# A linear-attention and gated MoE-style kernel: order of work listed anew, three sums moved to TensorE, four transfers moved to ScalarE's queue

## The chip, the cores and the metric

One core of one Trainium2 chip runs the whole program. The time is device microseconds of that core for one execution. Three executions of the kernel before took 303.40 to 303.96 us, median 303.87.

## The reference

Two stages follow each other. Inputs are float32 as the core sees them for the first stage; the weights of the second (`w_in`, `conv_w`, `w_out`) come as float64 and are split on the chip into a high and a low part.

```python
# first stage: 4 batches, 8 heads, 768 steps, head size 48
f = 1.0 / (1.0 + np.exp(-f_logit))
for t in range(S):
    state = f[:, :, t, :, None] * state + np.einsum('bhd,bhe->bhde', k[:, :, t], v[:, :, t])
    y[:, :, t] = np.einsum('bhd,bhde->bhe', q[:, :, t], state)
x = y.transpose(0, 2, 1, 3).reshape(B, S, 384)
# second stage
h = np.maximum(x @ w_in, 0.0)                       # 384 -> 1024
conv_out = sum(conv_w[k] * hp[:, k:k + S, :] for k in range(3))   # hp: h padded by one step
out = (h * (1.0 / (1.0 + np.exp(-conv_out)))) @ w_out            # 1024 -> 384
```

## The kernel before, in words

The steps of a batch are cut into six chunks of 128, so there are 24 chunks, numbered n; half a batch (three chunks, 384 steps) is the unit of the second stage, and there are eight of those, numbered u.

A chunk needs the running sum of the logarithms of its gates. The gates come in groups of three chunks. For the groups in `CFG["cg"]` they are loaded with time on the partitions (L493), ScalarE takes the logarithm (L505, L509), and TensorE sums by four matmuls with a triangle of ones (`cumulate`, L530). For the other groups the load has features on the partitions (L495) and VectorE runs a scan along time (L537). Two exponentials of the sum follow on ScalarE (L539, L541), and VectorE multiplies keys and queries by them (L545). TensorE then computes scores in four quarters of its array (L567), transposes the keys (L560), and multiplies keys by values (L595) and masked scores by values (L587). VectorE copies the scores through the mask (L575) and carries the state (L608, L611), which ScalarE decays (L617). TensorE adds queries times state (L631), and ScalarE and VectorE write the result as a high part and a remainder (L644, L646) into the tile `xT` of the half batch.

Heads have 48 rows of 64, so a quarter of each output would stay empty. Six gap transfers in each half batch (L654), from SBUF to SBUF, fill the gaps with rows of a fourth slot. They wait for the last remainder (L646) of the half batch, and the projection of the half batch waits for all six.

The second stage of a half batch: nine matmuls for each of eight blocks of `w_in` (L684, high and low parts), a halved relu (L694), three taps of the convolution (L700, L704), a tanh (L708), the product (L710), a split into high and low (L727, L731), 24 matmuls with `w_out` (L740), a copy (L746) and a store (L748).

The weights are split beside the first chunks by VectorE and ScalarE (`split_f64`, L390 to L436); two splits let TensorE join the parts by matmuls with the identity (L431 to L433), and the first projection waits for two of the three splits of `w_in`. In the end the weights are loaded once more to check that none is out of range (L760 to L766), and the count of good ones (L781, L782) decides on a slow path that does not run here.

Every step is an operation with needs, buffers and engine (`plan.op`). `ORDER`, a table of operation numbers, sets the sequence of each engine; `order` walks it with modelled times and hands out the buffers (`rings`) as they come free. All transfers are issued by SP, in the table's order; each waits for the transfer eight places ahead of it. In the model, `told`, `edge`, `asked` and `read` count TensorE's instructions against the places at which a new block of 256 has to be there. Before the sequence begins, seven matmuls on a zeroed tile keep TensorE busy (`STIR`, L368).

Of the kernel before, what the change touches and what calls it, by code (L numbers as in the profile page):

```python
# [11 lines left out]
F32 = mybir.dt.float32  # L12
# [40 lines left out]
845 716 809 722 367 120 123 797 379 836 323v 339 353 851 326 370 819 340 824 399 350 341 397 798 398 787 342 351 400  # L53
# [35 lines left out]
class Plan:  # L89
# [34 lines left out]

    def buf(self, i):
        return self.at[i]

    def order(self):
        now = 0.0
        free = {e: 800.0 for e in self.LAT}  # L130
# [21 lines left out]
        while events:  # L152
# [18 lines left out]
            for e in free:  # L171
# [8 lines left out]
                for o in [o for o in todo[e][:1] if o in ready[e]] if turn else sorted(ready[e], key=lambda o: o.key):  # L180
# [5 lines left out]
                    for r, i in o.take:  # L186
                        if not turn and r not in self.LOOSE and fifo[r][head[r]] is not o:
                            ok = False
                            break
# [768 lines left out]
```

## Time and profile before

| what | value |
|---|---|
| median of 3 executions | 303.87 us |
| the profiled execution | 303.62 us |
| its span, first to last instruction | 301.9 us |
| TensorE matmuls | busy 287.8 us, 95% |
| TensorE weight loads | busy 271.6 us, 90% |
| VectorE | busy 255.9 us, 85% |
| ScalarE | busy 243.4 us, 81% |
| GpSimd | busy 28.1 us, 9% |
| moved by transfers | 43.57 MB, mean 144 GB/s |

The profiled execution took 303.62 us; its span is 1.72 us shorter, which lies around the program's own instructions. PE is TensorE (PEld its weight loads), DVE is VectorE, ACT is ScalarE, POOL is GpSimd, and a q behind an engine's name stands for its sequencer, which waits and issues transfers. A float32 matmul is recorded as two passes, a transpose or a reduced-precision one as one. In the chain of waits, each row is what released the next; "issue" there, and as a releaser, is time for which the profile shows nothing that was waited for.

### The profile page before, as it was taken

What the parts mean: (1) busy time and instruction counts of PE and PEld (TensorE: products, weight loads), DVE (VectorE), ACT (ScalarE), POOL (GpSimd) and SP (SyncE); (2) the same over time, 40 slices, a digit from 0 to 9 for tenths busy, and PEclk for the clock granted to TensorE, in tenths of its full rate; (3) what the DMA queues carried; (4) which work ended last, traced back from release to release, by engine and by line L of the source; (5) the groups of instructions that cost most, each with busy time, mean ns of one, the idle gap of its engine ahead of it and who ended that gap; (6) DMA issues with size and microseconds to landing.
All of it is one profiled execution on the core that took longest, in us unless ns stands there. A gap on an engine that the chain in (4) does not pass through costs nothing.

```text
span 301.9 us, 10060 instructions
## 1 busy us (share of the span) xinstructions
PE 287.8 (95%) x4281; PEld 271.6 (90%) x4281; DVE 255.9 (85%) x394; ACT 243.4 (81%) x457; POOL 28.1 (9%) x72
## 2 busy tenths in 40 slices
PE   7668979999999999999999999999999999999994
PEld 6557667999999999999999999999999999999993
DVE  5959999999999999999999789995886698479530
ACT  6959788999678799899999778678989795796521
POOL 4003240002110010012000000020000002000000
PEclk9979999999999999999999999999999999999999
DMA  6996899542510344744361433553643505201211
GB/s 209 391 407 227 259 270 374 169 124 72 154 44 7 121 134 125 218 138 136 100 196 62 145 90 104 143 169 107 204 144 99 148 29 143 69 26 41 80 38 58
DMA packets 19476, 43.57 MB, mean 144 GB/s; under 512 B 2764, under 2 KB 9700, under 8 KB 19428
## 3 DMA queue, kind: packets, MB, share of 16 engines
q1 hardware_dynamic: 19428, 42.90, 44.3%
q8 instruction: 34, 0.56, 0.8%
q14 instruction: 14, 0.11, 0.1%
HBM read 35.81 MB, written 4.72 MB: 134 GB/s over the span
## 4 chain that ended last, share of the span: by engine, by line
PE 87%; DVE 5%; DMA 3%; issue 2%; SPq 1%; ACT 0%; DVEq 0%; ACTq 0%
PE mm L684 34%; PE mm L740 33%; PE Y L587 4%; PE S L567 3%; PE Y L631 3%; PE Y L595 3%; PE Y L560 3%; DVE kq L545 2%; DMA xT<-xT 2%; DMA xT<-in_moe_conv_w_dram 1%; SPq L654 1%; DVE ob L423 1%; DVE fb L537 1%; PE mm L530 1%; PE mm L431 1%
## 5 line engine op out<-in xcount | busy, mean ns | idle before, releaser
L684 PE MATMUL mm<-xT,wi 128*128 128x384 f32 x576 | 107.7, 341 | 1.5 <-DMA xT<-xT 1.5
L684 PEld LDWEIGHTS mm<-xT,wi 128*128 128x128 f32 x576 | 100.5, 188 | 2.9 <-ACT e L539 1.7
L704 DVE SCALAR_TENSOR_TENSOR g<-hb,cw,g 128x384 f32<-128x384 f32 (+1 forms) x128 | 73.5, 614 | 6.0 <-ACT g L700 5.6
L740 PE MATMUL mm<-wo,gh 128*128 128x384 f32 x384 | 71.0, 338 | 0.0
L740 PEld LDWEIGHTS mm<-wo,gh 128*128 128x128 f32 x384 | 66.4, 188 | 0.5 <-ACT gh L727 0.2
L700 ACT ACTIVATE g<-hb,cw 128x384 f32<-128x384 f32 (+1 forms) x64 | 37.8, 618 | 2.6 <-DVE gl L731 2.1
L694 ACT ACTIVATE hb<-mm 128x384 f32<-128x384 f32 x64 | 31.2, 488 | 10.7 <-PE mm L684 10.1
L731 DVE TENSOR_TENSOR gl<-g,gh 128x1024 fp32r<-128x1024 f32 (+2 forms) x28 | 29.6, 1067 | 10.8 <-ACT gh L727 7.2
L740 PE MATMUL mm<-wo,gl 128*128 128x384 f32 x192 | 37.4, 338 | 0.0
L740 PEld LDWEIGHTS mm<-wo,gl 128*128 128x128 f32 x192 | 33.3, 188 | 0.1
L727 ACT CAST gh<-g 128x1024 fp32r<-128x1024 f32 (+2 forms) x28 | 26.1, 938 | 7.8 <-PE mm L740 6.3
L710 DVE SCALAR_TENSOR_TENSOR g<-g,hb 128x768 f32<-128x768 f32 (+1 forms) x32 | 30.3, 956 | 1.7 <-ACT g L708 1.6
L708 ACT ACTIVATE g<-g 128x768 f32<-128x768 f32 (+1 forms) x32 | 27.0, 845 | 3.7 <-DVE g L704 3.6
L545 DVE TENSOR_TENSOR kq<-kq,e 128x1024 f32<-128x1024 f32 x24 | 29.1, 1216 | 0.1
L587 PE MATMUL Y<-am,v 64*48 64x64 f32 (+1 forms) x768 | 23.5, 219 | 2.5 <-issue 2.5
L543 POOL COPY ft_all<-e 128x4 f32<-128x4 f32 x24 | 14.1, 592 | 104.1 <-ACT e L541 104.0
L537 DVE TENSOR_TENSOR_SCAN fb<-runs,fb 128x512 f32<-128x512 f32 x18 | 21.8, 1217 | 0.4 <-ACT fb L509 0.3
L746 ACT COPY ob<-mm 128x384 f32<-128x384 f32 x24 | 11.4, 474 | 12.5 <-PE mm L740 6.3
L567 PE MATMUL S<-kq 48*64 48x64 f32 x768 | 16.9, 222 | 3.3 <-DVE kq L545 3.3
L575 DVE COPY_PREDICATED am<-mask,S 128x512 f32<-128x512 uint8 x24 | 17.6, 733 | 2.8 <-PE Y L587 2.8
L646 DVE TENSOR_TENSOR xT<-Y,xT 112x512 fp32r<-112x512 f32 x24 | 16.5, 687 | 2.5 <-ACT xT L644 2.4
L567 PEld LDWEIGHTS S<-kq 48*64 48x64 f32 x768 | 13.9, 134 | 5.2 <-DVE kq L545 3.7
(95 smaller groups left out, 362.2 us busy)
## 6 DMA issues: line engine op xcount, KB each, us to landing
kq<-in_kq_dram SPq DMA_DIRECT2D x24, 512.0 KB, 4.4
fb<-in_f_logit_dram SPq DMA_DIRECT2D x18, 256.0 KB, 4.8
v<-in_v_dram SPq DMA_DIRECT2D x24, 192.0 KB, 4.2
out_dram<-ob SPq DMA_DIRECT2D x24, 192.0 KB, 2.1
kq<-in_moe_w_out_dram SPq DMA_DIRECT2D x8, 384.0 KB, 3.7
kq<-in_moe_w_in_dram SPq DMA_DIRECT2D x6, 512.0 KB, 4.4
xT<-xT SPq DMA_DIRECT2D x48, 48.0 KB, 2.9
xT<-in_moe_w_in_dram SPq DMA_DIRECT2D x4, 512.0 KB, 7.9
```

The lines of the kernel that those rows point to most:

```text
L545: ox = plan.op("DVE", 1222, lambda e, X=X, E=E: nc.vector.tensor_tensor(buf(X), buf(X), buf(E), ALU.mult), ka, need=[o2, ld_x], use=[X, E])
L567: o = nc.tensor.matmul(scores()[t, j, p, :], buf(X)[r, 0, p, t], buf(X)[r, 1, p, t], start=True, stop=True)
L587: o = nc.tensor.matmul(out_of(Y, p, j, w, z), buf(V).rearrange("p h d -> p (h d)")[t, h * D:h * D + w], buf(AM)[t, j, p, :], start=x == 1 ...
L684: nc.tensor.matmul(buf(ph)[:, :HS], wi[:, t, wl, f * P:(f + 1) * P], x_view(pl, u)[:, t, xl, :], start=(i == 0), stop=(i == 3 * KT - 1))
L694: nc.scalar.activation(hb[:, 2:HS + 2], buf(ph)[:, :HS], AF.Relu, scale=0.5)
L700: o = pl.op("ACT", 620, lambda e, cv=cv, hb=hb, n=n, f=f: nc.scalar.activation(cv(), hb[:, 1:n + 1], AF.Copy, scale=cw[:, 1, f:f + 1]), ke ...
L704: o = pl.op("DVE", 617, lambda e, cv=cv, hb=hb, n=n, f=f, w=w, sh=sh: nc.vector.scalar_tensor_tensor(cv(), hb[:, sh:n + sh], cw[:, w, f:f ...
L708: o = pl.op("ACT", 846, lambda e, cv=cv: nc.scalar.activation(cv(), cv(), AF.Tanh), key, need=last, use=[("g", u)], mode="T")
L710: gates[u, fp] = pl.op("DVE", 960, lambda e, cv=cv, fp=fp, n=n: nc.vector.scalar_tensor_tensor(cv(), cv(), 1.0, h_b[:, fp:fp + 2, 1:n + 1] ...
L727: o = pl.op("ACT", 180 + 110 * nn * NF // 128, lambda e, hv=hv, src=src: nc.scalar.copy(hv(), src()), key, need=[gates[v, fp] for fp in ra ...
L731: los.append(pl.op("DVE", 150 + 134 * nn * NF // 128, lambda e, hv=hv, lv=lv, src=src: nc.vector.tensor_tensor(lv(), src(), hv().bitcast(F ...
L740: nc.tensor.matmul(buf(po)[:, :DM], view(g)[:, f, :], wo[:, f, wl, :], start=(i == 0), stop=(i == 3 * NF - 1))
```

## The change

The table `ORDER` is written anew for all engines, and its entries now carry the buffer as well as the operation, so that nothing is modelled in the built program (`fixed`). In the planner the count of TensorE's instructions starts with those of the stir matmuls and the first block ends at 186 instead of 192. The group of chunks 6 to 8 joins `cg`: its sums are made by TensorE from loads of 192 KB, and its three scans on VectorE go. Seven stir matmuls of 128 columns become two of 512. In the first half batch, three of the six gap transfers are issued by ScalarE. The copy of an output tile may be put on VectorE (three of 24 are), one key copy and one state decay more go there too, and the very last store is issued by ScalarE. The check of the weights reads twelve pieces of 512 instead of six of 512 and eight of 384.

```diff
-STIR = 7
+STIR = 2
 MID, HALF = 1024.0, 126.0
...
-CFG = dict(cap=9999, lf=3, sg=3, cg=(0, 1), nf=6, groups=[3, 3, 3, 3, 3, 3, 3, 3], f=(-172.297, 32.759), gate=(-21.55,
+CFG = dict(cap=9999, lf=3, sg=3, cg=(0, 1, 2), nf=6, groups=[3, 3, 3, 3, 3, 3, 3, 3], f=(-172.297, 32.759), gate=(-21.55,
...
 ORDER = """
-79 80 33 97 131 81 82 99 83 149 84 132 133 98 85 34 167 35 151 36 134 37 135 38 39 100 40 136 685 101 137 152 86 239
...
+79.0 80 33.0 88.1 81 131.0 82 132.0 83.0 149.1 84 11.1 133.0 12 90 134.0 150.1 85.1 89 86 151.1 135 136 137 167.2
...
+    def fixed(self):
+        done = []
+        for w in ORDER.split():
+            i, _, k = w.partition(".")
+            o = self.ops[int(i.rstrip("v"))]
+            o.on = "DVE" if i[-1] == "v" else next(iter(o.engs))
+            for r, t in o.take:
+                o.spot.append((t, self.rings[r][int(k)][0]))
+            done.append(o)
+        assert sorted(map(id, done)) == sorted(map(id, self.ops))
+        return done
+
     def order(self):
+        if self.tuned and ORDER.strip():
+            return self.fixed()
...
-        sent, flown, told, edge, read, asked = [], 0, 0, 192, 0.0, 0.0
+        sent, flown, told, edge, read, asked = [], 0, 4 * STIR if self.tc else 0, 186, 0.0, 0.0
...
-                seen = o.end + self.LAT[e]
+                seen = o.end + self.LAT[e] + (o.size if e == "ACT" else 0)
...
-        nc.tensor.matmul(plan.rings["mm"][i % 2][0][:, :P], stir, stir, start=True, stop=True)
+        nc.tensor.matmul(plan.rings["mm"][i][0].rearrange("p (n t) -> p n t", t=P), stir,
+                         stir.rearrange("p (n t) -> p n t", n=1).broadcast_to([P, WC // P, P]), start=True, stop=True)
...
-                gathered[u].append(plan.op("SP", 560, lambda e, u=u, t=t, s0=s0, d0=d0: nc.sync.dma_start(
+                e, ns, size = ("ACT", 450, 2000) if u == 0 and j else ("SP", 560, 48)
+                gathered[u].append(plan.op(e, ns, lambda e, u=u, t=t, s0=s0, d0=d0: (nc.scalar if e == "ACT" else nc.sync).dma_start(
                     x_view(plan, u)[d0:d0 + GAP, t, :, :].bitcast(F32), x_view(plan, u)[s0:s0 + GAP, KT, :, :].bitcast(F32)),
-                    (3 * u + 2, "ga"), need=[x_done[3 * u + k] for k in range(CPH)], use=[("xT", u)], size=48))
+                    (3 * u + 2, "ga"), need=[x_done[3 * u + k] for k in range(CPH)], use=[("xT", u)], size=size))
...
-                o = pl.op("ACT", 489, lambda e, ob=ob, po=po: nc.scalar.copy(buf(ob), buf(po)[:, :DM]), key, need=[o],
+                o = pl.op(dict(ACT=489, DVE=355), 0, lambda e, ob=ob, po=po: (
+                    nc.scalar.copy if e == "ACT" else nc.vector.tensor_copy)(buf(ob), buf(po)[:, :DM]), key, need=[o],
                           use=[po], take=[("ob", ob)])
-                pl.op("SP", 400, lambda e, ob=ob, b=b, m=m: nc.sync.dma_start(out[b, m * P:(m + 1) * P, :], buf(ob)), key,
-                      need=[o], use=[ob], size=192)
...
+    n_w = 12
+    far = const.tile([P, n_w], F32, name="far")
...
-    for i, src in enumerate(halves):
-        w, n, key = ("kq", ("w", i)), src.shape[-1], N + 2.0 + 0.2 * i
-        raw = lambda w=w, n=n: plan.buf(w[1]).rearrange("p a n t -> p (a n t)")[:, :2 * n]
+    flat = [w.rearrange("(p r) n -> p (r n)", p=P) for w in (w_in, w_out)]
+    for i in range(n_w):
+        src = flat[i // 6][:, i % 6 * WC:(i % 6 + 1) * WC]
+        w, key = ("kq", ("w", i)), N + 2.0 + 0.2 * i
+        raw = lambda w=w: plan.buf(w[1]).rearrange("p a n t -> p (a n t)")
```

Line numbers move by 13 to 20. Three places of the built order follow.

**VectorE, chunks 0 to 2.** `kq` are keys and queries of a chunk (the number is the buffer), `fb` the gates whose scan is printed as SCALAR_TENSOR_TENSOR with `runs`, `am` the masked scores, `sh` and `st` the state, `gh`, `gl` and `ob` parts of a weight split. Before:

```order
L545 TENSOR_TENSOR kq0_113<-kq0_113,e0_121 128x1024
L537 SCALAR_TENSOR_TENSOR fb1_112<-runs_81,fb1_112 128x512
L575 COPY_PREDICATED am0_89<-mask1_86,S_108 128x512
L545 TENSOR_TENSOR kq1_114<-kq1_114,e1_122 128x1024
L537 SCALAR_TENSOR_TENSOR fb1_112<-runs_81,fb1_112 128x512
L575 COPY_PREDICATED am1_90<-mask1_86,S_108 128x512
L545 TENSOR_TENSOR kq2_115<-kq2_115,e0_121 128x1024
L611 TENSOR_TENSOR st1_94<-Y0_109,sh0_95 112x192
L537 SCALAR_TENSOR_TENSOR fb1_112<-runs_81,fb1_112 128x512
L575 COPY_PREDICATED am0_89<-mask1_86,S_108 128x512
L646 TENSOR_TENSOR xT5_327<-Y0_109,xT5_327 112x4x128
L395 TENSOR_SCALAR gh8_341<-xT3_218 128x1024
```

Now:

```order
L558 TENSOR_TENSOR kq1_114<-kq1_114,e1_122 128x1024
L624 TENSOR_TENSOR st1_94<-Y0_109,sh0_95 112x192
L424 SCALAR_TENSOR_TENSOR gl3_201<-xT0_141,gl3_201 24x128
L426 TENSOR_TENSOR c32_133<-gh2_173,gl3_201 24x128
L588 COPY_PREDICATED am1_90<-mask1_86,S_108 128x512
L408 TENSOR_SCALAR gh5_272<-xT1_151 128x1024
L411 SCALAR_TENSOR_TENSOR gh5_272<-xT1_151,gh5_272 128x1024
L659 TENSOR_TENSOR xT6_294<-Y0_109,xT6_294 112x4x128
L421 TENSOR_SCALAR gl7_330<-gh5_272 128x1024
L621 TENSOR_TENSOR sh1_96<-Y1_110,st1_94 112x192
L478 COPY cw_107<-mm0_129 128x24
L558 TENSOR_TENSOR kq2_115<-kq2_115,e0_121 128x1024
```

The three scans are gone, the split of the first piece of `w_in` (L408, L411, L421, in the old numbering L395, L398, L408) stands ahead of the third product of keys and queries, and the masked copy of chunk 2 comes behind both.

**TensorE, around its 445th instruction (weight loads and matmuls counted; a row x16 of 64x64 is 64 of them).** `Y` is the chunk's output bank, `S` the scores, `tri` the triangle of ones. Before, with the 445th in the last-but-one row:

```order
L567 MATMUL S<-kq_115 64x64 x16
L631 MATMUL Y_109<-kq_113,sh_95 48x64
L631 MATMUL Y_109<-kq_113,sh_95 64x64 x2
L631 MATMUL Y_109<-kq_113,sh_95 48x64 x2
L631 MATMUL Y_109<-kq_113,sh_95 64x64 x2
L631 MATMUL Y_109<-kq_113,sh_95 48x64
L587 MATMUL Y_109<-am_89,v_117 48x64
L587 MATMUL Y_109<-am_89,v_117 64x64 x2
L587 MATMUL Y_109<-am_89,v_117 48x64 x2
L587 MATMUL Y_109<-am_89,v_117 64x64 x2
L587 MATMUL Y_109<-am_89,v_117 48x64
L530 MATMUL mm_129<-tri_74,fg_125 128x128 x4
```

Now, with the 445th in the first rows of `am_90`:

```order
L608 MATMUL Y_110<-v_118,kp_123 64x48
L608 MATMUL Y_110<-v_118,kp_123 48x48
L600 MATMUL Y_110<-am_90,v_118 48x64
L600 MATMUL Y_110<-am_90,v_118 64x64 x2
L600 MATMUL Y_110<-am_90,v_118 48x64 x2
L600 MATMUL Y_110<-am_90,v_118 64x64 x2
L600 MATMUL Y_110<-am_90,v_118 48x64
L543 MATMUL mm_129<-tri_74,fg_125 128x128 x4
L573 MATMUL Y_109<-ident,kq_115 128x128 x4
L580 MATMUL S<-kq_115 64x64 x16
```

The carried products of chunk 0 (L631, L587 of `Y_109`) and a further sum now lie ahead of this place, and the value products of chunk 1 are at it; behind it stand, as before, a sum and the transposes and scores of chunk 2.

**SP and ScalarE, the gap transfers of the first half batch.** Before, all on SP (`xT<-xT`):

```order
L519 DMA kq_115<-in_kq_dram 128x1024
L495 DMA fb_111<-in_f_logit_dram 128x512
L654 DMA xT_327<-xT_327 16x768 x3
L443 DMA xT_592<-in_moe_w_out_dram 128x768
L654 DMA xT_327<-xT_327 16x768 x2
L495 DMA fb_111<-in_f_logit_dram 128x512
L654 DMA xT_327<-xT_327 16x768
L443 DMA g_335<-in_moe_w_out_dram 128x768
L521 DMA v_118<-in_v_dram 128x384
```

Now on SP:

```order
L456 DMA g_504<-in_moe_w_in_dram 128x1024
L668 DMA xT_294<-xT_294 16x768
L456 DMA g_504<-in_moe_w_in_dram 128x1024
L668 DMA xT_294<-xT_294 16x768 x2
L456 DMA g_400<-in_moe_w_out_dram 128x768 x2
L534 DMA v_119<-in_v_dram 128x384
L508 DMA fb_112<-in_f_logit_dram 128x512 x3
```

and on ScalarE:

```order
L657 CAST xT_294<-Y_109 112x4x128
L522 ACTIVATE fg_126<-fb_111 128x8x48
L449 CAST wi<-mm_130 128x512
L584 COPY kp_123<-Y_110 128x512
L668 DMA xT_294<-xT_294 16x768
L552 ACTIVATE e_121<-mm_129 128x512
L668 DMA xT_294<-xT_294 16x768
L554 ACTIVATE e_121<-mm_129 128x512
L449 CAST wi<-mm_130 128x512
L584 COPY kp_123<-Y_109 128x512
L416 ACTIVATE wo<-gh_532 128x2x384
L668 DMA xT_294<-xT_294 16x768
```

Three of the six stand on ScalarE between exponentials (`e`), weight copies (`wi`, `wo`) and key copies (`kp`); on SP one load of a weight stands between the three that stayed, and the loads of gates and of `w_out` come behind them.

## Rows read from the trace of the kernel before

**Rows 1.** The page: engines, granted clock in 40 slices, instruction queue

```profile
PE 287.8 (95%) x4281; PEld 271.6 (90%) x4281; DVE 255.9 (85%) x394; ACT 243.4 (81%) x457; POOL 28.1 (9%) x72
...
PEclk9979999999999999999999999999999999999999
...
q8 instruction: 34, 0.56, 0.8%
```

**Rows 2.** Busy time by stretch: us, PE, PEld, DVE, ACT, POOL, PEclk, DMA share, GB/s

```profile
42.00:60.00 18.00, 18.00 (x312) 15.66 (x311) 17.38 (x26) 16.22 (x28) 3.78 (x1) 1.00 0.83 278
60.00:90.00 30.00, 30.00 (x431) 28.61 (x430) 29.74 (x52) 25.43 (x52) 4.92 (x9) 1.00 0.34 99
```

**Rows 3.** Waits of TensorE: in total, times, longest (us)

```profile
PE S L567 <- DVE kq L545: 3.3, 3, 2.1
PE Y L587 <- issue: 2.5, 1, 2.5
PE mm L684 <- DMA xT<-xT: 1.5, 1, 1.5
PE mm L368 <- DVE stir L295: 1.2, 1, 1.2
PE Y L631 <- DVE st L611: 0.7, 1, 0.7
PE mm L530 <- ACT fg L509: 0.5, 1, 0.5
```

**Rows 4.** The chain of waits, 8 to 42 us: start, us, what

```profile
15.67 2.49 issue
...
32.90 0.62 SPq L654
...
36.57 5.02 DMA xT<-xT
...
41.72 0.41 PE mm L684
```

**Rows 5.** Timeline of the end: start, us, what

```profile
296.76 1.72 SPq L748 DMA_DIRECT2D out_dram<-ob  x2
...
297.50 0.19 PE L781 MATMUL S<-ones,oks 128*1 128x1 f32 x2
297.65 0.48 ACT L746 COPY ob<-mm 128x384 f32<-128x384 f32 x1 [0.91 <-PE mm L740]
```

**Rows 6.** Busy time by stretch around the wait at 15.67

```profile
15.70:18.20 2.50, 0.04 (x1) 0.00 (x0) 0.17 (x1) 0.00 (x0) 0.00 (x0) 1.00 1.06 415
18.20:22.50 4.30, 4.09 (x61) 3.47 (x60) 3.24 (x6) 3.53 (x10) 0.00 (x0) 0.60 1.04 406
```

**Rows 7.** Timeline of VectorE, 7 to 19 us: start, us, what, idle before

```profile
8.66 1.22 DVE L537 TENSOR_TENSOR_SCAN fb<-runs,fb 128x512 f32<-128x512 f32 x1
...
14.65 1.22 DVE L537 TENSOR_TENSOR_SCAN fb<-runs,fb 128x512 f32<-128x512 f32 x1
18.46 0.73 DVE L575 COPY_PREDICATED am<-mask,S 128x512 f32<-128x512 uint8 x1 [2.59 <-PE Y L587]
```

**Rows 8.** Timeline of TensorE: one chunk's sum (eight passes)

```profile
9.91 1.11 PE L530 MATMUL mm<-tri,fg 128*128 128x128 f32 x8
```

**Rows 9.** Line 530, the sums: duration min/median/max in ns

```profile
L530 PE MATMUL mm<-tri,fg x48: 275/275/579, 4.5 to 24.5; 128*128 128x128 f32 x48
```

**Rows 10.** The whole chain of waits: nine projection matmuls at two places

```profile
56.81 1.57 PE mm L684 x9
...
64.87 1.79 PE mm L684 x9
```

**Rows 11.** Line 654, the gap transfers: issue in ns, time to landing

```profile
L654 SPq DMA_DIRECT2D xT<-xT x48: 507/581/1399, 32.9 to 238.8; - x48
...
DMA to landing us min/median/max: 2.0/2.9/5.4
```

**Rows 12.** The page: issues of the stores, KB, us to landing

```profile
out_dram<-ob SPq DMA_DIRECT2D x24, 192.0 KB, 2.1
```

More of the change, by code (lines that the diff above doesn't have):

```diff
@@ L35 @@
 ORDER = """
[17 rows of a table removed]
-845 716 809 722 367 120 123 797 379 836 323v 339 353 851 326 370 819 340 824 399 350 341 397 798 398 787 342 351 400
[4 rows of a table removed]
-439 584 907 434 129 581 393v 870 910 583 409 425 794 470 582 471 410 856 875 580 911 895 579 876 900 449 422 857 882
[6 rows of a table removed]
-966 981 510 941 500 657 511v 1033 530 499v 1007 501 539 986 514 967 502 1008 531 543 658 515 603 516 1039 594 1009 968
[14 rows of a table removed]
[5 rows of a table added]
+20.1 183 208 227 105.1 239.0 21 184 193.0 209 29.1 555 556 1 240.0 559 181v 558 46.0 210.0 241 557 45.0 196 30 52 47
[14 rows of a table added]
+322 380.3 836 119 708 323v 123 841 778 367 120 798 338 352.0 339 324 815 803 340 325 344.0 816 789.0 781.1 811 379.2
[9 rows of a table added]
+473 907 938.0 967.0 505 956 456.1 968 446 489 457v.0 476.0 908 447 503.3 460 963 523 974 911 490 975.0 969 472 964 461
+965 943 980.1 944 976 917.1 462 448 912 913.0 477.1 586 981 506.0 589 918.1 970 971 914 463v 491 474.0 945 464 475.0
+966 494.0 524.1 504.0 957 478 465.1 588 507 919.1 466 915.1 508 479 977 480 509 972 929.0 495.0 920 939 973 492.1
+930.0 482 493.0 982 512.0 940 521.0 951 496 978 587 483 513.1 931.0 916 525 585 541 481 526 590 946 484 923.1 497 947
+510.0 932 498 999 511.0 921v.0 499v 1025 983 958 500 514 501 607.1 1031.1 933.1 515 502 527 594 603.2 1000.0 1032 595
+516 984 522.2 924.0 518 979 530.0 539.3 528.1 952 985 593 1005.1 953 591 1001 529v.0 540.1 608 922 519.2 925.0 1002.1
[14 rows of a table added]
 """
@@ L137, in order @@
         seq = 0
-        turn = [(int(w.rstrip("v")), w[-1] == "v") for w in ORDER.split()] if self.tuned else []
-        todo = {e: [] for e in self.LAT}
-        for k, (i, v) in enumerate(turn):
-            o = self.ops[i]
-            e = "DVE" if v else next(iter(o.engs))
-            o.engs, o.key = {e: o.engs[e]}, (k, i)
-            todo[e].append(o)
         done, dma, pipe, mode, table = [], [], 0.0, None, "NE"
-        sent, flown, told, edge, read, asked = [], 0, 0, 192, 0.0, 0.0
+        sent, flown, told, edge, read, asked = [], 0, 4 * STIR if self.tc else 0, 186, 0.0, 0.0
         for o in self.ops:
@@ L179, in order @@
                     flying = sum(o.size for o in sent[flown:])
-                for o in [o for o in todo[e][:1] if o in ready[e]] if turn else sorted(ready[e], key=lambda o: o.key):
+                for o in sorted(ready[e], key=lambda o: o.key):
                     spot = {}
@@ L186, in order @@
                     for r, i in o.take:
-                        if not turn and r not in self.LOOSE and fifo[r][head[r]] is not o:
+                        if r not in self.LOOSE and fifo[r][head[r]] is not o:
                             ok = False
@@ L202, in order @@
                         ready[x].remove(o)
-                if turn:
-                    todo[e].pop(0)
                 for r, i in o.take:
@@ L277, in gla_moe_kernel @@
     WC = 512
+    LAST = (B - 1, CPH - 1)
     steps = [(b, c) for b in range(B) for c in range(NC)]
@@ L745, in moe @@
                 o = pl.op("PE", 1388, lambda e, mm2=mm2: mm2(e, z=1), key, need=[o] + los, use=[gl, po], mode="r", n=16)
-                o = pl.op("ACT", 489, lambda e, ob=ob, po=po: nc.scalar.copy(buf(ob), buf(po)[:, :DM]), key, need=[o],
+                o = pl.op(dict(ACT=489, DVE=355), 0, lambda e, ob=ob, po=po: (
+                    nc.scalar.copy if e == "ACT" else nc.vector.tensor_copy)(buf(ob), buf(po)[:, :DM]), key, need=[o],
                           use=[po], take=[("ob", ob)])
-                pl.op("SP", 400, lambda e, ob=ob, b=b, m=m: nc.sync.dma_start(out[b, m * P:(m + 1) * P, :], buf(ob)), key,
-                      need=[o], use=[ob], size=192)
+                end = "ACT" if extra and (b, m) == LAST else "SP"
@@ L751, in gla_moe_kernel @@
+                pl.op(end, 400, lambda e, ob=ob, b=b, m=m: (nc.scalar if e == "ACT" else nc.sync).dma_start(
+                    out[b, m * P:(m + 1) * P, :], buf(ob)), key, need=[o], use=[ob], size=192)
     halves = [w_in[k * P:(k + 1) * P, z * WC:(z + 1) * WC] for k in range(KT) for z in range(2)]
     halves += [w_out[f * P:(f + 1) * P, :] for f in range(NF)]
-    far = const.tile([P, len(halves)], F32, name="far")
+    n_w = 12
+    far = const.tile([P, n_w], F32, name="far")
     mid = const.tile([P, 1], F32, name="mid")
@@ L759, in gla_moe_kernel @@
         hi = lambda raw=raw: raw().rearrange("p (n w) -> p n w", w=2)[:, :, 1]
         o = plan.op("SP", 430, lambda e, raw=raw, src=src: nc.sync.dma_start(raw().bitcast(I32), src.bitcast(I32)), key,
-                    take=[w], size=n)
-        o = plan.op("ACT", 160 + 0.908 * n, lambda e, hi=hi: nc.scalar.activation(hi(), hi().bitcast(I32), AF.Abs, scale=2.0 ** -20),
+                    take=[w], size=512)
+        o = plan.op("ACT", 625, lambda e, hi=hi: nc.scalar.activation(hi(), hi().bitcast(I32), AF.Abs, scale=2.0 ** -20),
@@ L771, in gla_moe_kernel @@
         plan.trace()
-    n_ft, n_w = B * NC * NP, len(halves)
+    n_ft = B * NC * NP
     ok = const.tile([P, n_ft + n_w], F32, name="ok")
```

4 lines of the change are left out of this document (2 added, 2 removed), and 81 rows, old and new, of the table ORDER.

## The prediction

> **What bounds the kernel now.** I read the page's busy shares first: TensorE is busy 287.8 of 301.9 us and the granted clock is full except in the third of the forty slices [rows 1]. The split by stretch then shows where the rest is: from 42 us on TensorE is busy in every microsecond of a stretch, 18.00 of 18 and 30.00 of 30, while VectorE reaches 17.38 and 29.74 of the same [rows 2]. So after 42 us the end moves only with TensorE's own work, and VectorE is close behind it. What TensorE waits for stands in its waits: 9.7 us in all, every one of them before its first projection matmul (L684) at 41.72 us [rows 3, 4]. The span is therefore TensorE's work, plus 9.7 us of waits in the first 42 us, plus the 4.2 us between its end (297.69) and the span's [rows 5]. A gain has to come out of those waits, since the change adds work.
>
> The chain of waits names the two places that matter. At 15.67 TensorE stops for 2.49 us and no releaser is found ("issue") [rows 3, 4]. It had then executed 222 matmuls and as many weight loads, 444 instructions; the instruction queue moved 34 transfers of 16 KB (0.56 MB) [rows 1], and 2 x 4281 instructions over 34 make some 252 a transfer, so 444 is near the end of a second one. In that stretch the data queues are full: DMA share 1.06 [rows 6]. I read it as a block of instructions that arrived late behind data. VectorE loses 2.59 us there, from the third sum to the third masked copy [rows 7], and afterwards TensorE runs 18.2 to 22.5 at a granted clock of 0.60 on the mean, so mostly at 1.2 GHz instead of 2.4, after it had sat idle for those 2.5 us [rows 6]. The second place is the gather of the first half batch: VectorE finishes it at 32.9, SP then issues six gap transfers between other loads, and the one that releases L684 is issued at 36.57 and lands 5.02 us later [rows 4].
>
> **The change part by part.**
>
> *Nine chunks' sums on TensorE instead of six.* Three more sums of four matmuls (eight passes each). A sum takes 1.11 us with the tail of its last pass [rows 8], and one pass 0.275 [rows 9]; by the pitch of the passes, (1.11 - 0.275) / 7 x 8 = 0.95 us behind other work. Three of them: 2.85 us taken, 3.3 at most, all on the path if the waits do not swallow them. In exchange VectorE loses three scans of 1.22 us, which the kernel before ran between 8.66 and 15.87, in its most crowded stretch [rows 7]: 3.7 us at most. These chunks' loads are 192 KB instead of 256 KB.
>
> *Order of TensorE's work.* By the two listings, changes between the quarter-array matmuls (chunks) and the full ones (projections, joins) fall from 38 to 32, those to or from transposes and sums rise from 53 to 61. Nine projection matmuls take 1.57 us behind a transpose and 1.79 behind scores [rows 10], so a change is worth up to 0.22; six fewer give 0 to -1.3, and the eight more of the other kind, whose price no row shows alone, take some of it back. I take -0.5. TensorE's work thus grows by 2.85 - 0.5 = 2.35 us.
>
> *The waits before 41.72.* There are six [rows 3]. The 1.5 us for the gather should go: SP keeps three gap transfers with one load among them, about four issues of 0.58 [rows 11], so its last starts 1.8 us after the gather while the releasing one started 3.7 us after it [rows 4]; with 2.0 to 5.4 us to land [rows 11] the last is there 7.2 us after the gather at worst, and I expect the gather itself some 3 us earlier, by the scans alone. 1.5 us go (bounds 0 and 1.5). Of the 2.49 us I keep most. The listing puts the 445th instruction into chunk 1's value products instead of chunk 0's, so TensorE has the sum of chunk 3 and the conv-weight transpose done by then, but it also gets there no later than before, and the queues are as full. What changes is the cover: VectorE now has most of a weight split ready at that point, where before it had nothing. Yet the next transpose needs the third product of keys and queries, which VectorE now does after that split, so part of the wait returns as a wait for VectorE. I take 0.9 us gone (bounds -1 and 2.5). Of the 3.3 us before the scores, 2.1 (the first load) stay and 0.7 of the other 1.2 go; the 0.7 for the state sum and the 0.5 for the gates go, since scans and 256 KB loads stand ahead of neither any more. Together 1.5 + 0.9 + 0.7 + 0.7 + 0.5 = 4.3 us of 9.7.
>
> *The clock.* 4.3 us at 0.60 cost 1.7 us against the full clock [rows 6]. With a shorter wait I take 0.6 us back (bounds 0 and 1.7).
>
> The Trainium skill (Runtime: NRT & Kernel Launch, Instruction fetch mechanics) says that crossing a block of 256 instructions is mostly hidden, and by it placing work around blocks would be worth nothing. The trace agrees for all blocks but one; the one wait of 2.49 us speaks against it.
>
> *Three gap transfers on ScalarE.* Each holds ScalarE for an issue (0.51 to 1.40 us on SP [rows 11]), and the first stands there waiting for VectorE's gather with an exponential, a weight copy and a key copy queued behind it. Some 1.8 to 3 us of ScalarE, in a stretch where it is not the latest; price on the path 0 to 2 us, taken as 0. If ScalarE is late, the joins and TensorE's L684 are late next.
>
> The Trainium skill (DMA: Bandwidth & Descriptors, Issuing engines are not separate DMA queues) says a second issuing engine saves only issue time, usually small beside the transfer. Here the issues from the gather to the releasing transfer take 3.7 us beside a landing of 5.0, so the trace disagrees on "small"; by the rule this term would be near 0 and the total about 302.4.
>
> *The last store on ScalarE.* The last copy ends at 298.13, SP issues the store until 298.48 and only then takes part in the closing steps [rows 5]. ScalarE can issue it right behind its own copy, and SP is free 0.33 us sooner. The landing (2.1 us [rows 12]) is the same, so 0 to 0.5; taken 0.2.
>
> *The rest.* Two stir matmuls of 512 columns for seven of 128 are done before the first sum's data, as before: 0. Twelve checks of the weights instead of fourteen, three output copies, one key copy and one decay moved to VectorE: nearly all after 42 us, on engines with slack; they cost nothing while VectorE keeps its gaps (0.6 of 18, 0.3 of 30 [rows 2]), and if that cover goes TensorE waits there.
>
> **Sum.** +2.35 - 4.3 - 0.6 - 0.2 = -2.75. The profiled execution took 303.62 us, 0.25 below the median of 303.87: 303.62 - 2.75 = **300.9 us**. With each unknown at its good end (order 0.8 more, block wait 1.6, clock 1.1, last store 0.3): 297.1. At its bad end (sums 0.45 and order 0.5 dearer, gather 1.5 back, block wait 1.9 worse, clock 0.6 and store 0.2 back, ScalarE's issues 2.0): 308.0. Either needs them all together.
>
> **Rivals.**
>
> *The block wait goes fully and the clock stays up.* For it: VectorE's scans are gone, and the order is new around that place. Against: TensorE reaches it as early as before and the loads ahead are as many. Then 1.6 and 1.1 us more: 300.9 - 2.7 = 298.2. Chance 0.15.
>
> *The head is no shorter.* The waits shift (ScalarE stands at its gap transfers, the third product comes late), and only what the added sums cost is won back: 2.35 of waits gone instead of 4.3, no clock gain: 303.62 - 0.2 = 303.4. This is also the case in which the change doesn't do what it says at the blocks: were the 2.49 us no matter of blocks, it would recur wherever the loads are thickest. The Trainium skill's rule on hidden crossings (Runtime: NRT & Kernel Launch, Instruction fetch mechanics) would lead here. Chance 0.12.
>
> *Slower: new block waits where TensorE is full.* After 42 us every block arrives in time now (one "issue" wait in the whole view [rows 3]). The new order packs the chunks' matmuls differently; where two blocks pass in quarter-array work while loads are thick, a wait of 2.49 plus a slow stretch of 1.7 us costs 4.2 us, fully on the path. One such wait eats the gain (305.1); it decides from the first. For it: the new sequence crosses blocks inside chunk work about as often. Against: 33 of 34 crossings are free now. Chance 0.11.
>
> *ScalarE or VectorE starves TensorE behind L684.* TensorE is 2.8 us earlier there, VectorE by its scans 3.7 us at most; if it is late by half of TensorE's lead, 1.4 us come back as waits between 42 and 60: 302.3. Chance 0.17.
>
> **How the numbers follow.** My forecast has 0.45, the fast rival 0.15, the starved one 0.17: faster than before by over 0.2% (0.6 us, about what a measurement of this kernel can tell) 0.77. The shorter head that isn't: 0.12, same. The new block waits: 0.11, slower. The range should leave out 2 in 10: it reaches down to the fast rival, 298.2, and up to 303.4, which takes in the starved case and the unchanged head and leaves the block waits out.
>
> **What would show it.** TensorE's waits sum to some 5.4 us, the one for the gather is gone and L684 starts near 39; the "issue" wait stands in chunk 1's value products with VectorE busy beside it; 42 us on is without a wait; the sums are 72 passes. An "issue" wait after 45 us, a gather wait as long as before, or ScalarE idle ahead of its gap transfers while TensorE waits would make the forecast wrong.

## The result and the profile after

| | before | after |
|---|---|---|
| median | 303.91 us (303.4 to 305.14, 6 runs) | 307.46 us (306.25 to 308.43, 6 runs) |
| ratio | 1 | 1.0109, 95% interval 1.0079 to 1.0140 |
| profiled execution | 303.62 us, span 301.9 | 307.80 us, span 306.1 |
| TensorE's last work ends | 297.69 us | 301.93 us |
| first projection matmul | 41.72 us | 42.87 us |

The change made the kernel 1.1% slower; the forecast was 1.0% faster. Ratios, here and below, leave out executions more than 1.5% above the fastest of their kernel (three of six in run 1, one of twelve each in runs 7 and 12, two of the 35 of the kernel before that stand beside runs 9 to 12). The page of the kernel after, engines, granted clock in 40 slices, and two queues (q10 is ScalarE's own):

```profile
PE 292.2 (95%) x4295; PEld 274.8 (90%) x4295; DVE 254.8 (83%) x392; ACT 239.6 (78%) x447; POOL 33.3 (11%) x72
...
PEclk9789999999999999999999999999999999999998
...
q8 instruction: 34, 0.56, 0.8%
q10 hardware_dynamic: 240, 0.34, 0.3%
```

Beside [rows 1]: TensorE is busy 4.4 us longer, VectorE and ScalarE 1.1 and 3.8 us less, and GpSimd, of which the forecast never spoke, 5.2 us longer with the same 72 instructions. The waits of TensorE in the kernel after (in total, times, longest, us):

```profile
PE mm L698 <- ACT hb L708: 2.2, 1, 2.2
PE mm L543 <- ACT e L554: 1.3, 2, 1.1
PE mm L380 <- DVE stir L307: 1.2, 1, 1.2
PE Y L600 <- issue: 1.1, 1, 1.1
PE mm L543 <- ACT fg L522: 1.1, 1, 1.1
PE S L580 <- DVE kq L558: 1.0, 1, 1.0
PE mm L543 <- DVE cw L478: 0.8, 1, 0.8
PE Y L608 <- ACT kp L584: 0.4, 1, 0.4
PE mm L445 <- issue: 0.3, 1, 0.3
PE mm L698 <- ACT wi L449: 0.2, 1, 0.2
```

Beside [rows 3], the scores' wait fell from 3.3 to 1.0, the wait without a releaser from 2.5 to 1.1, and the wait for the gather is gone. Yet the sum is 9.6 us, as before (9.7): new waits stand in their place. Three of them (2.2, 0.4 and 0.3) lie behind the first projection, where the kernel before had none. The busy time by stretch shows that (us, PE, PEld, DVE, ACT, POOL, granted clock, DMA share, GB/s):

```profile
42.00:60.00 18.00, 17.01 (x233) 14.45 (x233) 16.59 (x24) 15.42 (x27) 0.63 (x2) 1.00 0.77 262
60.00:90.00 30.00, 27.79 (x492) 26.01 (x491) 27.34 (x47) 25.48 (x54) 6.05 (x6) 1.00 0.40 115
```

In [rows 2] TensorE had 18.00 and 30.00 there. Now each new wait, with its lines.

**GpSimd under VectorE (2.2 us).** The timeline of the kernel after around 78 us (start, us, what, and in brackets the idle time before and its releaser):

```profile
78.15 4.88 POOL L688 COPY hb<-hb 128x4 f32<-128x4 f32 x2 [5.85 <-DVE g L724]
...
78.54 4.33 DVE L718 SCALAR_TENSOR_TENSOR g<-hb,cw,g 128x385 f32<-128x385 f32 x8
...
82.94 0.49 ACT L708 ACTIVATE hb<-mm 128x384 f32<-128x384 f32 x1 [3.39 <-POOL hb L688]
...
83.49 0.79 PE L698 MATMUL mm<-xT,wi 128*128 128x384 f32 x3 [2.21 <-ACT hb L708]
```

GpSimd copies two columns of the relu's halo. The first of these two copies takes 4.76 us beside eight VectorE operations without a gap, and ends 0.05 us after the last of them (82.86). ScalarE's relu must not overwrite the columns, so it waits 3.39 us, and TensorE 2.21. Eleven of the other fifteen copies take 0.18 to 0.52 us, the remaining four 1.12 to 2.65; of the ten copies over 0.4 us, nine end 0.04 to 0.05 us behind the end of a VectorE operation. The Trainium skill (SBUF — State Buffer, SBUF: two separate sides) says that VectorE and GpSimd share a pair of ports under an exclusive lock: against a GpSimd operation that reads SBUF, a VectorE operation with two SBUF inputs that starts first holds it for the whole instruction, and the other side blocks. The trace agrees, and shows besides that eight such operations in a row did not let the copy in between (it is recorded from 0.39 us before the first of them, when VectorE was at another operation).

**ScalarE's order in the head (1.2 us).** ScalarE from 4 to 10 us in the kernel after:

```profile
4.30 0.51 ACT L518 ACTIVATE fb<-fb 128x384 f32<-128x384 f32 x1
6.74 0.60 ACT L552 ACTIVATE e<-mm 128x512 f32<-128x512 f32 x1 [1.93 <-PE mm L543]
7.23 0.51 ACT L522 ACTIVATE fg<-fb 128x384 f32<-128x384 f32 x1
...
8.06 0.59 ACT L554 ACTIVATE e<-mm 128x512 f32<-128x512 f32 x1
```

The second gate's logarithm (L522) now stands behind the first exponential (L552), which waits 1.93 us for TensorE's first sum. TensorE then waits 1.1 us for that logarithm, and the first scores start at 9.96 us instead of 8.80. The kernel before waited 2.1 us for its scores here too [rows 3], so the two waits of 1.10 and 1.00 us are not 2.1 us more: what is lost at this place is the 1.16 us by which the scores come later.

**ScalarE at its third gap transfer (1.1 us).** ScalarE from 32 to 41 us in the kernel after:

```profile
32.78 0.63 ACTq L668 DMA_DIRECT2D xT<-xT  x1
...
35.99 0.84 ACT L416 ACTIVATE wo<-gh 128x768 fp32r<-128x768 f32 x1
38.84 0.51 ACTq L668 DMA_DIRECT2D xT<-xT  x1
39.40 0.52 ACT L518 ACTIVATE fb<-fb 128x384 f32<-128x384 f32 x1 [2.57 <-DMA xT<-xT]
```

The chain of waits has "32.78 6.04 DMA xT<-xT" here: the third issue on ScalarE waited until its first gap transfer had landed, a gate and two exponentials queued behind it, and the last of the three added sums behind these. Counted over both queues, the third is the eighth transfer behind the first, and the program makes each transfer wait for the one eight places ahead of it. On SP such a wait stops only other transfers; on ScalarE it stops its computing too. In the kernel before, SP had issued the last gap transfer earlier:

```profile
37.84 0.51 SPq L654 DMA_DIRECT2D xT<-xT  x1
```

**The clock (1.7 us).** The kernel before had one stretch of 3.4 us at 1.2 GHz inside TensorE's work, this execution has two:

```profile
10.80:14.20 3.40, 3.40 (x52) 3.17 (x54) 1.80 (x3) 1.76 (x4) 0.19 (x1) 0.50 1.04 409
...
21.00:24.40 3.40, 3.40 (x59) 3.07 (x62) 2.70 (x5) 2.13 (x5) 0.00 (x0) 0.50 0.34 129
```

Each comes behind a pair of waits: 1.10 and 1.00 us of idle before 10.8, 1.13 and 0.79 before 21.0. Such a pair isn't always followed by a fall: the profiled execution of run 4 has the same 1.10 and 1.00 us, ending at 7.16 and 9.32 us, and full clock until 18.9. Over its six runs the mean granted clock is 0.979 to 0.991; 17 later runs of the kernel before have 0.983 to 0.994.

### The profile page after: what moved, and what is told of

It is laid out like the page before. It is cut to its first block, busy times and chain, and to the rows that moved or that the text cites. A ratio compares the mean times of both kernels' runs of the same rounds, so it can differ in the third digit from the quotient of the medians.

```text
span 306.1 us, 10041 instructions
## 1 busy us (share of the span) xinstructions
PE 292.2 (95%) x4295; PEld 274.8 (90%) x4295; DVE 254.8 (83%) x392; ACT 239.6 (78%) x447; POOL 33.3 (11%) x72
## 4 chain that ended last, share of the span: by engine, by line
PE 80%; ACT 12%; DMA 2%; DVE 2%; POOL 2%; issue 1%; ACTq 0%; DVEq 0%; POOLq 0%
PE mm L754 33%; PE mm L698 27%; PE Y L573 3%; PE Y L644 3%; PE S L580 3%; PE Y L600 3%; PE Y L608 3%; PE mm L543 2%; DMA xT<-xT 2%; ACT st L630 2%; POOL hb L688 2%; ACT g L714 1%; PE mm L380 1%; ACT hb L708 1%; ACT fb L518 1%
## 5 line engine op out<-in xcount | busy, mean ns | idle before, releaser
L688 POOL COPY hb<-hb 128x4 f32<-128x4 f32 x16 | 16.1, 1013 | 98.4 <-DVE g L724 98.4
L600 PE MATMUL Y<-am,v 64*64 64x64 f32 (+1 forms) x768 | 23.3, 220 | 1.1 <-issue 1.1
L556 POOL COPY ft_all<-e 128x4 f32<-128x4 f32 x24 | 13.1, 558 | 82.2 <-ACT e L554 82.2
L600 PEld LDWEIGHTS Y<-am,v 64*48 64x48 f32 (+1 forms) x768 | 18.7, 128 | 1.3 <-issue 1.3
L550 DVE TENSOR_TENSOR_SCAN fb<-runs,fb 128x512 f32<-128x512 f32 x15 | 18.1, 1214 | 0.0
```

The costliest lines, as they stand in the source:

```text
L600: o = nc.tensor.matmul(out_of(Y, p, j, w, z), buf(V).rearrange("p h d -> p (h d)")[t, h * D:h * D + w], buf(AM)[t, j, p, :], start=x == 1 ...
```

## The experiments

Two theories. *Waits*: the new sequence made waits of its own, each at a named place; without them the change is worth something. *Work*: the added sums are simply on the path, and what is taken from one wait comes back in the next. Every kernel was timed against the kernel before on the same chip.

**1. The sums back on VectorE.**

```diff
-CFG = dict(..., cg=(0, 1, 2), ...
+CFG = dict(..., cg=(0, 1), ...
```

> The changed kernel with the sums of chunks 6, 7 and 8 back on VectorE as scans, at the same places of the sequence. If the added sums are work on the path and nothing swallows them: 2.85 us less TensorE work, 307.5 - 2.85 = 304.6 us (304.0 to 305.5). If the head is set by waits for VectorE and ScalarE and not by TensorE's work, the three scans (3.7 us of VectorE) give it back: 306.8 to 308.

Measured: 308.66, 311.02 and 313.14 us, ratio 1.0244 (1.0193 to 1.0294), by the ratios some 4.1 us more than with the sums on TensorE. Neither number was right; the sign is that of the second alternative. TensorE waited for VectorE and the copies behind it at places where the kernel after doesn't (three of its waits; the profiled execution, 313.80 us, is one of its longest):

```profile
PE Y L644 <- DVE st L624: 3.2, 2, 1.7
...
PE Y L573 <- DVE kq L558: 1.0, 1, 1.0
...
PE mm L444 <- ACT wi L449: 0.7, 1, 0.7
```

So in this sequence three scans of 1.2 us on VectorE, with the larger loads that go with them, cost more than the sums. What the sums cost by themselves this run can't show, since the scans stand in their places.

**2. The logarithm first.** The order table, op 85 (logarithm) ahead of 134 (exponential), 135 right behind it:

```diff
-... 133.0 12 90 134.0 150.1 85.1 89 86 151.1 135 136 137 ...
+... 133.0 12 90 85.1 134.0 150.1 135 89 86 151.1 136 137 ...
```

> The changed kernel with one thing moved on ScalarE: the logarithm of chunk 1's gate stands before the first exponential of chunk 0, and the second exponential of chunk 0 right behind the first, as in the kernel before. If the waits of 1.10 and 1.00 us between 6.7 and 10 us and the stretch at 1.2 GHz behind them (10.8 to 14.2, 1.7 us lost) come from this place: the first scores start near 9.0 instead of 9.96, no 1.2 GHz stretch before the block wait, 304.5 to 306 us. If the loads or the block wait at the 445th instruction take it up: over 306.8 us, with a longer block wait.

Measured: 306.20 us (304.91 to 308.26), ratio 1.0095 (1.0060 to 1.0129): 1.3 us lower by the median, though the interval overlaps that of the kernel after. The wait for the logarithm went and no 1.2 GHz stretch came before the block wait (run 4 has none there either, with the waits in place); the one behind it lasted 6.83 us instead of 3.41. The scores still started at 9.7 instead of 9.96, since VectorE's first product had another late input:

```profile
8.45 1.23 DVE L558 TENSOR_TENSOR kq<-kq,e 128x1024 f32<-128x1024 f32 x1 [4.61 <-DMA kq<-in_kq_dram]
```

The new order of loads puts two gates' loads ahead of the first keys and queries.

**3. All six gap transfers on SP.**

```diff
-e, ns, size = ("ACT", 450, 2000) if u == 0 and j else ("SP", 560, 48)
+e, ns, size = ("SP", 560, 48)
```

> The changed kernel with all six gap transfers of the first half batch issued by SP again. If ScalarE's stand of 2.0 us at its third gap transfer (36.83 to 38.84 in the profile) is what delays the last sum and the first projection: the 1.10 us wait at 40.4 and the 0.2 at 42.7 go, the first projection starts 0.5 to 1.3 us earlier unless the sixth transfer lands later, 306.2 to 307.0 us. If the transfers' landing sets the projection's start, SP's serial issues (0.58 each) put it 1 to 2 us later: 307.5 to 309 us.

Measured: 308.37 us (305.67 to 310.25), ratio 1.0141 (1.0090 to 1.0192). Unclear against the kernel after; if anything slower. The 1.10 us wait went, and 0.8 us of waiting for a transfer came at the projection: what ScalarE lost, the landing took.

**4. The halo copies on VectorE.**

```diff
-oe = pl.op("POOL", 620, lambda e, fp=fp: nc.gpsimd.tensor_copy(h_b...
+oe = pl.op("DVE", 90, lambda e, fp=fp: nc.vector.tensor_copy(h_b...
```

> The changed kernel with the sixteen copies of two columns (relu halo, L688) on VectorE behind the gate instead of on GpSimd. If GpSimd's copy of 4.76 us at 78.15 beside eight VectorE operations back to back is what TensorE waited for at 81.28 (2.21 us): that wait goes, 307.5 - 2.2 = 305.3 us (304.8 to 306). If VectorE is itself the later one there, sixteen more operations on it give nothing: 307 to 308 us, and TensorE waits for VectorE in 78 to 90.

Measured: 304.65 us (302.99 to 305.92, 12 runs), ratio 1.0016 (0.9989 to 1.0044): 2.8 us less, with intervals well apart, and 0.6 more than the wait of 2.2 us. The sixteen copies now take 0.15 to 0.18 us each, and the wait for ScalarE's relu is gone from the waits. Waits without a releaser ("issue") stand in five places instead of two, 5.2 us in this execution instead of 1.4:

```profile
PE Y L600 <- issue: 1.7, 1, 1.7
PE mm L445 <- issue: 1.6, 1, 1.6
...
PE mm L698 <- issue: 0.9, 1, 0.9
...
PE Y L608 <- issue: 0.7, 1, 0.7
PE Y L644 <- issue: 0.3, 1, 0.3
```

**5 and 6. Two, then three edits at once.** Run 5 has the edits of runs 2 and 4; run 6 also moves the first load of keys and queries (op 131):

```diff
-79.0 80 33.0 88.1 81 131.0 82 ...
+79.0 80 33.0 131.0 81 88.1 82 ...
```

> Both edits at once: the logarithm of chunk 1's gate first, and the halo copies on VectorE. If the two waits are independent pieces of the path, their gains add: 307.46 - 2.8 - 1.3 = 303.4 us (302.8 to 304.2). If the head's gain is taken up behind it (block waits, loads), the result stays at that of the halo copies alone: 304.3 to 305 us.

> As the run before it, and the first load of keys and queries (512 KB) issued ahead of the gates of chunks 2 and 3 instead of behind them, so that it is the fourth load and not the sixth. In the run with the logarithm first, the first product of keys and queries started at 8.45 us, when that load landed, and not when its exponentials were ready (7.0). If the order of the loads is the second half of the late head: first scores near 8.8 us instead of 9.7 and 1 us less than the run before it, 302.4 us (301.8 to 303.2), below the kernel before. If the block wait at the 443rd instruction or VectorE takes it up: within 0.3 us of the run before it, with a longer wait there.

Measured: run 5 303.62 us (301.66 to 305.68), ratio 0.9984 (0.9953 to 1.0014); run 6 303.79 us (301.65 to 304.40), ratio 0.9967 (0.9938 to 0.9995), where the kernel before had 304.36 beside them. The gains of runs 2 and 4 add, within their intervals; of the 1 us of the load's place a part at most arrived. Run 6's first scores start at 8.57 us, as forecast, but its waits show where it went:

```profile
PE S L580 <- DVE kq L558: 1.8, 1, 1.8
PE Y L600 <- issue: 1.3, 1, 1.3
PE Y L608 <- issue: 1.2, 1, 1.2
...
PE mm L445 <- issue: 1.0, 1, 1.0
...
PE Y L644 <- issue: 0.6, 1, 0.6
PE mm L446 <- issue: 0.4, 1, 0.4
```

Five waits without a releaser, 4.5 us.

**7. Twenty instructions more ahead of the sequence.** With the edit of run 4:

```diff
-STIR = 2
+STIR = 7
...
-nc.tensor.matmul(...[i][0].rearrange(...), stir, stir....broadcast_to([P, WC // P, P]), ...)
+nc.tensor.matmul(...[i % 2][0][:, :P], stir, stir, ...)
```

> The halo copies on VectorE, and seven stir matmuls of 128 columns instead of two of 512, so that TensorE has 40 instructions more (20 matmuls, 20 weight loads) ahead of the same sequence. If the waits without a releaser belong to instruction blocks, they stay at the same counts (near 443 and 1715) and so move 40 instructions earlier in the program: from chunk 1's value products into its rank products (L608), and from the weight join at 48.7 us into the chunk work before it. If they belong to a place in the program (loads thick there), they stay in those operations, at counts near 483 and 1755. Time: 304.6 us if one place is as good as the other, 305.5 to 306.5 if the sequence was fitted to the blocks and now isn't.

The trace has ten matmuls (4305 for 4295) and ten weight loads more, so the edit adds twenty instructions, not forty, and the places of the second alternative would be 463 and 1735. Measured: median 305.91 us (303.69 to 307.56), ratio 1.0043 (1.0014 to 1.0072), by the ratios 0.8 us more than run 4, with intervals that overlap. Two of its waits (its lines are numbered one lower than above; the profiled execution, 308.31 us, is its longest):

```profile
PE Y L599 <- issue: 1.6, 1, 1.6
...
PE Y L607 <- issue: 0.3, 1, 0.3
```

Counted in the trace, they stand again ahead of TensorE's instructions 443 and 1715, but in other operations: the first in the rank products (L607, in the kernel after L608) instead of the value products, the second in value products instead of the weight join (L445). So the waits belong to instruction counts. Every wait without a releaser over 0.25 us in the runs of the new sequence falls at one of 443, 697 or 699, 953, 1209, 1461 or 1463, 1715: 252 to 256 apart. In each that could be matched, the 16 KB of the instruction queue had ended 1.2 to 1.6 us before TensorE went on (in the kernel after 17.95, then 19.38; 49.69, then 51.02). The queue had begun to move that block at most some 180 instructions before TensorE stopped (in the kernel before only at 15.76 us, 0.09 us after the stop), and quarter-array products use those up in a fraction of that time. Which crossings cost something differs between executions of one order: at 697 the profiled executions of runs 4 and 6 wait 0.7 and 1.2 us, those of the kernel after and of run 11 (the order of run 6 up to there) not at all.

**8. The halo copies of the kernel before on VectorE.**

```diff
-nc.gpsimd.tensor_copy(h_b...
+nc.vector.tensor_copy(h_b...
```

> The kernel before, with its halo copies on VectorE. TensorE waits for none of them there (the longest took 2.04 us and nobody waited), so if the copy matters only where TensorE waits for it: within 0.3 us of the kernel before. If GpSimd's copies cost VectorE time too, or the clock has more to do with it: 302.5 us or less.

Measured: 303.73 us (303.21 to 306.01), ratio 0.9990 (0.9962 to 1.0017). No difference: the copies cost nothing where nobody waits for them.

**9 and 10. Slow pieces ahead of the crossings.** Run 9 is run 6 with chunk 4's sum (op 205) ahead of chunk 1's rank products (160), and what the sum needs (93, 94, 42) earlier; run 10 also moves a weight join (18) ahead of chunk 2's rank products (178):

```diff
-... 13.0 168.2 146 97.0 14 41.0 147.0 185.0 160 221.3 93 99 148 94.0 145 15.0 95 161 16 42 173 205.0 162 ...
+... 13.0 93 94.0 168.2 146 97.0 14 41.0 42 147.0 185.0 221.3 99 148 145 15.0 95 205.0 160 161 16 173 162 ...
...
-... 25 178 44 100 186.1 96.1 18.0 98
+... 25 18.0 178 44 100 186.1 96.1 98
```

> The run with three edits (first load of keys and queries early, logarithm first, halo copies on VectorE), and chunk 4's sum (32 slow instructions) moved ahead of chunk 1's rank products, its gate ahead of ScalarE's xT copy and the conv weights' copy ahead of VectorE's other work, so that TensorE crosses the 443rd instruction some 32 instructions earlier in the program, right behind a sum. If the block's instructions come a fixed time after TensorE nears them, the sum covers them: the wait of 1.25 us falls to under 0.4 and the 0.73 us wait for the conv weights' copy goes, 0.7 to 1.4 us less than that run, some 0.994 of the kernel before. If the fetch is late for the loads alone, the wait stays at 1.2 us or more: no gain, 0.997 of the kernel before.

> As the run before it, and the first weight join (8 slow instructions) moved ahead of chunk 2's rank products, in which the second block wait lies (1.23 us at the 697th instruction). If a slow piece ahead of the crossing covers the fetch: that wait falls to 0.6 us or less, 0.4 to 0.8 us less than the run before it. If VectorE sets that stretch (chunk 2's state comes 1 us later): same as the run before it, or up to 0.5 us more.

Measured: run 9 302.84 us (301.88 to 304.12), ratio 0.9949 (0.9925 to 0.9974), the lowest median here; run 10 303.19 us (302.45 to 304.11), ratio 0.9960 (0.9932 to 0.9988), the same within the intervals. Against run 6 the gain isn't certain either. The waits tell more; run 9's, then run 10's:

```profile
PE Y L573 <- DVE kq L558: 1.7, 1, 1.7
...
PE Y L608 <- issue: 1.1, 1, 1.1
PE mm L543 <- DVE cw L478: 1.0, 1, 1.0
```

```profile
PE Y L573 <- DVE kq L558: 1.8, 2, 1.7
...
PE mm L543 <- ACT st L630: 1.0, 1, 1.0
PE mm L698 <- issue: 0.6, 1, 0.6
```

In run 9 the wait at 443 is gone (no L600), that at 699 stays; in run 10 that one is gone too, and one of 0.6 us stands at 1463. At 443 every other profiled execution of the new sequence waits, 0.3 to 2.2 us, so there the sum (sixteen instructions in the trace, not 32) covered the block, together with the 1.0 us that TensorE waits just ahead of it. At 699 one execution shows little, since run 11 has no wait there without the edit. And VectorE, now behind with the third product, takes back 1.7 us in both. Part of run 9's gain may be the clock: in eleven of its twelve executions the mean granted clock is 0.996 or more (the profiled one has 0.988), in run 6 the median is 0.994.

**11 and 12. The gap transfers, alone.** Run 11 is run 6 with all six on SP (the edit of run 3). Run 12 is the kernel before with three on ScalarE and nothing else:

```diff
-gathered[u].append(plan.op("SP", 560, lambda ...: nc.sync.dma_start(
+e, ns = ("ACT", 450) if u == 0 and j else ("SP", 560)
+gathered[u].append(plan.op(e, ns, lambda ...: (nc.scalar if e == "ACT" else nc.sync).dma_start(
```

> The run with three edits, with all six gap transfers on SP. There ScalarE no longer stands at its third one, so what is left is the issue time. If three transfers on ScalarE are worth what was forecast (the last gap transfer starts 1.8 us earlier): the first projection starts 1 us or more later, with a wait, 0.5 to 1.5 us slower than that run. If the landing hides it: within 0.3 us of it.

> The kernel before, with three gap transfers of its first half batch on ScalarE and nothing else. If the forecast term holds alone, the wait of 1.46 us at 40.27 goes and the first projection starts 1 to 1.5 us earlier: 0.995 to 0.997 of the kernel before. If ScalarE's issues (0.5 each, and a wait for its own earlier transfer) delay the copies and exponentials behind them, TensorE waits for ScalarE instead: 0.999 or more.

Measured: run 11 304.55 us (302.05 to 306.53), ratio 1.0007 (0.9977 to 1.0036) against run 6's 0.9967: 1.2 us by the ratios, with intervals that overlap. The traces don't settle it: the profiled execution of run 11, its shortest, waits 1.3 us in the first projection, but began that at 38.93 us, run 6's at 41.06. The view names a load of gates; the sixth gap transfer, issued at 36.37 us, landed at 41.35, just ahead of the matmul that waited (41.49).

```profile
PE mm L698 <- DMA fb<-in_f_logit_dram: 1.3, 1, 1.3
```

Run 12: median 306.02 us (304.45 to 308.48), ratio 1.0052 (1.0020 to 1.0084), slower. The wait for the gather went, but not because the transfers came sooner: the last was issued at 39.67 us (before 37.84) and the first projection started at 44.92 (before 41.72). ScalarE stood, as in the kernel after, at its second gap transfer until a load of keys and queries eight places ahead had landed (38.45) and at its third until its own first had (39.65):

```profile
35.58 0.58 ACT L436 CAST wi<-mm 128x512 fp32r<-128x512 f32 x1
38.48 2.13 ACTq L655 DMA_DIRECT2D xT<-xT  x2
40.65 1.01 ACT L617 ACTIVATE st<-st,ft_all 112x48 f32<-112x48 f32 x4 [4.50 <-DMA xT<-xT]
...
42.04 0.58 ACT L571 COPY kp<-Y 128x512 f32<-128x512 f32 x1
```

TensorE waited 3.13 us for that key copy ("PE Y L595 <- ACT kp L571: 3.1" in its waits). So three issues on ScalarE cost 1.6 us where ScalarE has to stand. That they win 1.2 us where it doesn't (in run 6 the third is issued at 34.47 us without a wait) isn't clear of the noise.

## Why the prediction was wrong

The terms, in the two profiled executions (us):

| term | forecast | found |
|---|---|---|
| three sums (0.89, 1.00 and 1.16 from their start to the next operation's) | +2.85 | +3.1 |
| waits up to the first projection, 9.7 to 6.7 | -4.3 | -3.0 |
| waits behind it | 0 | +2.9 |
| clock, a second stretch of 3.4 us at half speed | -0.6 | +1.7 |
| last store | -0.2 | 0.0 |
| fewer changes of array form (found: all that remains; no run shows the term alone) | -0.5 | -0.5 |
| sum, TensorE's end 297.69 to 301.93 | -2.75 | +4.2 |

Of the 7.0 us between the two sums, 2.9 are waits behind the first projection, 2.3 the clock and 1.3 the waits up to it. The two longer stir matmuls, taken as 0, let the first sum start 0.26 us later (4.79 us for 4.53).

*Right in kind.* The added work and the place of the first block wait (chunk 1's value products, VectorE busy beside it) came as forecast, and the head's waits shrank by 3.0 us, inside the bounds. Run 7 shows the reading of 15.67 us as a late block of instructions to be right: the wait keeps its count and changes its operation. Only the working was off: two transfers of 252 end at 504, not at 444; the planner's first block of 186 and 256 more give 442. The Trainium skill (Runtime: NRT & Kernel Launch, Instruction fetch mechanics) says that such a crossing is mostly hidden; most of the 34 are, and those in quarter-array work or right behind it cost 0.3 to 2.5 us here.

*Right by luck: the gather wait.* It ended, but its working didn't come out. SP's first gap transfer was issued at 32.77 us, not some 3 us before 32.90: taking the scans off VectorE did not bring the gather forward. SP's last was issued 3.1 us behind it and not 1.8, ScalarE's last at 38.84 us, 1.0 us later than the last of the kernel before. That one landed at 44.09 us, and TensorE, 1.15 us later than before at its first projection (42.87 us, forecast near 39), came to the matmul that needs it just then (44.22).

*The step that failed most: "they cost nothing while VectorE keeps its gaps", and "42 us on is without a wait".* The prediction counted the gaps of VectorE and ScalarE there and left out GpSimd, whose copies run only when VectorE lets them. One of them in front of TensorE cost 2.2 us, and moving them was worth 2.8 (run 4). The row was to be had: the same copy took up to 2.04 us in the kernel before, with nobody waiting. The rival of a starved TensorE behind the first projection had the right place and sign of the mechanism, with 1.4 us and two other engines.

*The clock.* "With a shorter wait I take 0.6 us back" took the one long wait for the cause. Two waits of about 1 us close together were followed by the same stretch, twice, and in run 4 one such pair was not; what else decides it stays open.

*ScalarE.* "Price on the path 0 to 2 us, taken as 0": run 12 measures the gap issues alone at +1.6 us in the old order. The bounds' reasoning priced the issues and the first one's wait for the gather, and left out that each transfer waits for the one eight places ahead, though the kernel before has that rule. The order of ScalarE's first five operations was not looked at at all; by the medians it cost 1.3 us (run 2), which isn't clear of the noise.

*The rival of new block waits* came true in part: they do appear at 1715 and elsewhere, 0.3 to 1.6 us each and not 4.2, and in run 6 they sum to 4.5 us. The *last store* moved nothing that shows: from the end of the last copy to the end of the span it is 3.77 us before and 3.70 after.

The cure of three places turns 1.0109 into 0.9967 (run 6), 4.3 us, so most of the loss was waits of the new sequence. Only the halo copies' part of it, 2.8 us, is shown by itself. That the change would then be worth 2.75 us is not borne out: 1.0 us is left, 1.5 in run 9. How much of each run's time the clock takes stays open; it differs from execution to execution of one kernel.

## What to carry to other kernels

Before a new order is trusted, list for every engine, GpSimd and the DMA-issuing queues too, what stands behind each instruction that may wait; a wait in front of a queue is priced by what queues, not by the instruction. A transfer that moves to a computing engine takes its waits along, that for an earlier transfer too. Keep small copies off GpSimd where VectorE runs two-input operations back to back and someone waits for them. Where an engine uses up many short instructions in little time, look for waits without a releaser at equal instruction counts, and try slow instructions ahead of them, if the next engine can bear it; here that removed a wait, and what it gained isn't clear of the noise.

## What the runs showed of the hardware

- A two-column copy on GpSimd took 4.76 us beside eight VectorE operations without a gap, 0.18 to 0.52 us in eleven other places, and 0.15 to 0.18 us on VectorE.
- TensorE went on 1.2 to 1.6 us after the packets of an instruction block had ended, and stopped at fixed counts whatever operation stood there.
- The granted clock fell to half for 3.41 or 6.83 us behind some waits and not behind others like them: a wait of 2.2 us for the halo copy was followed by a fall in run 3 (84.85 us) and by none in the kernel after, a pair of 1.10 and 1.00 us by a fall in the kernel after and by none in run 4.
- Moved to ScalarE, a transfer that had to wait for the one eight places ahead of it, counted over SP's and ScalarE's queues, held ScalarE until that had landed: 38.82 us, the issue at 38.84.
